# A head's q, k and guard rows together in DRAM, three V tiles moved into the score loop, the bound moved behind the last q block

## The chip, the core and the metric

The kernel runs on one core of one Trainium2 chip. The metric is the device time of one execution in microseconds (us). The engines named below are PE (TensorE), DVE (VectorE), ACT (ScalarE), POOL (GpSimd) and SP (SyncE, whose queue issues nearly all DMA transfers). The arithmetic in question is float32; matrix operands are split into a high and a low part of a shorter float type, and three products (high by high, high by low, low by high) stand in for one exact product.

## What is computed

One token block, 2048 rows of 512, goes through softmax attention with 32 heads of 16 columns, through a gated feed-forward layer of width 1792, and the two are mixed by a sigmoid gate:

```python
x = A_x                                             # 1 x 2048 x 512
g = sigmoid((x * gate_w).sum(-1, keepdims=True))
q, k, v = split(x @ wqkv)                           # 32 heads of 16
a = (softmax(q @ k.T * 16 ** -0.5) @ v) @ wo        # by head, heads side by side again
b = (silu(x @ w1) * (x @ w3)) @ w2
out = g * a + (1 - g) * b
```

## The kernel before

**First stage (lines 351 to 415).** `x` is loaded in four blocks of 512 rows, transposed on PE and split into `xH` and `xL`. For each block `project_qk` computes q and k of the first 8 heads; ACT copies the high half `hi`, DVE subtracts to get `lo`, and `store_qk` writes both to DRAM tensors of 512 rows (`QD`: qH, qL, kH, kL). `project_v` and `sums_v` compute the 16 tiles of V, twelve full-array matmuls each. `squares`, `x_squares`, `bound` and `guard_rows` work out an upper bound on the scores; two guard rows per head, written to `M_d`, become rows 48 and 49 of the q operand, so that the exponent can't overflow. If the bound is too large, a branch (`row_maxima`) computes true maxima; with these inputs it is not taken.

**The score loop (lines 849 to 880).** A string of letters fixes the order on PE. `Q` is `score`: two matmuls of 50 rows by 512 columns, one for each head of a pair, on the two halves of the array, and an exponential on ACT. `P` is `pv`: four matmuls of p with V into `acc`. `F` is `feed`: one matmul on each half of the array out of a list of other work (`blocks`: the rest of q and k, the feed-forward products, the output products). One long cycle `one` holds 8 Q, 21 F and 4 P; one short cycle `two` holds 8 Q, 15 F and 4 P. There are 90 long and 37 short cycles before the last one. A step is one pair of heads by one half of the queries, 32 Q; its operands `Qt` (q high, low, high and the guard rows: 50 rows by 1024) and `Kt` (k high, high, low: 48 rows by 2048, with rows of -1 behind them) are fetched by `load_step` one step ahead. Only the first step's operands are fetched ahead of the loop (lines 396, 401 and 409).

**The end (lines 882 to 953).** The last head pair is normalized on the spot; the last output products, eight tiles, run on PE with multiply-adds behind them and go out by DMA.

What sets the order is the program: each engine takes its instructions in the order written. On SP this holds for every DMA; each fetch or store waits there for what it needs.

Of the kernel before, what the change touches and what calls it, by code (L numbers as in the profile page):

```python
# [17 lines left out]
P = 128  # L18
# [4 lines left out]
DH = 16  # L23
NB = S // 512
# [9 lines left out]
def gated_mix_kernel(ctx: ExitStack, tc: tile.TileContext, x, wqkv, wo, w1, w3, w2, gate_w, out):  # L34
# [27 lines left out]
    qkp = ctx.enter_context(tc.tile_pool(name="qkp", bufs=1))  # L62
    fw = ctx.enter_context(tc.tile_pool(name="fw", bufs=2, side="right"))
# [3 lines left out]
    wvp = ph1.enter_context(tc.tile_pool(name="wvp", bufs=1))  # L67
# [112 lines left out]
    def x_gate(b):  # L180
        for t in range(4):
            nc.vector.scalar_tensor_tensor(slot("hx", F32), xn[b][:, t, :], 1.0, gw, op0=OP.mult, op1=OP.mult,
                                           accum_out=z[:, 4 * b + t:4 * b + t + 1])

    def store_qk(i, c, b, hi, lo):
        for t, d in zip((hi, lo), QD[i]):
            nc.sync.dma_start(d[P * c:P * c + P, 512 * b:512 * b + 512], t.bitcast(F32) if t.dtype == F32R else t)

    def project_qk(c, b, w, between=None):
        ps = psum2()  # L190
        for i in range(2):
            if i and between:
                between()
            order = [(h, xs, k) for h, xs in ((0, xH), (1, xH), (0, xL)) for k in range(ND)]
            if c == b == i == 0:
                order = [(0, xH, 0), (0, xH, 3), (0, xH, 1), (0, xH, 2), (0, xL, 0), (0, xL, 3),
                         (1, xH, 0), (1, xH, 3), (1, xH, 1), (1, xH, 2), (0, xL, 1), (0, xL, 2)]
            for n, (h, xs, k) in enumerate(order):
                nc.tensor.matmul(ps[:, i, :], w[i][h][:, k, :], xs[b][:, k, :], start=n == 0,  # L199
                                 stop=n == len(order) - 1)  # L200
        hi = p1.tile([P, 2, 512], F32R, name="hi", bufs=2)
        lo = p1.tile([P, 2, 512], F32R, name="lo", bufs=2)
        nc.scalar.activation(hi, ps, AF.Copy)
        nc.vector.tensor_sub(lo, ps, hi)
        for i in range(2):
            store_qk(i, c, b, hi[:, i, :], lo[:, i, :])
# [3 lines left out]
    def load_v():  # L210
        for k in range(ND):
            r = slot(("fh1", "fl1", "fh3", "fl3")[k], F32)
            nc.sync.dma_start(r, wqkv[P * k:P * k + P, 2 * D:3 * D])
            vh, vl = (wvp.tile([P, 512], F32R, name=f"v{n}{k}") for n in "hl")
# [37 lines left out]
    def guard_rows():  # L252
# [8 lines left out]
        for a in range(2):  # L261
            nc.sync.dma_start(M_d[:, a, :].rearrange("h (j t) -> h j t", t=512),
                              r[a][:].bitcast(F32)[:, None, :].to_broadcast([H, 4, 512]))
# [8 lines left out]
    def load_q(j, half, i):  # L272
        for h in range(2):
            r = 64 * h
            s = slice(DH * (2 * j + h), DH * (2 * j + h) + DH)
            for o, qs in enumerate((0, 1, 0)):
                nc.sync.dma_start(Qt[i][r + DH * o:r + DH * o + DH, :].bitcast(F32),
                                  QD[0][qs][s, 1024 * half:1024 * half + 1024])

    def load_guard(j, half, i):  # L280
        for h in range(2):
            nc.sync.dma_start(Qt[i][64 * h + 48:64 * h + 50, :].bitcast(F32),
                              M_d[2 * j + h, :, 1024 * half:1024 * half + 1024])

    def load_step(s):
# [3 lines left out]
        load_guard(j, half, s % 2)  # L289

    def row_maxima(small):

        with tc.If(small < 1):
# [4 lines left out]
            for j in range(NPAIR):  # L298
                load_k(j, 0)
                mx = p1.tile([P, 2, NT, 2], F32, name="mx")  # L300
                for t in range(NT):
                    if t % 8 == 0:
                        load_q(j, t // 8, 0)
# [16 lines left out]
                for h in range(2):  # L320
                    nc.sync.dma_start(M_d[2 * j + h].rearrange("a (t q) -> t a q", q=P),
# [116 lines left out]
    def qk_done(c, i, b):  # L438
        def done(ps):
# [6 lines left out]
            store_qk(i, c, b, hi, lo)  # L446
# [75 lines left out]
    def load_piece(t, q):  # L522
        if t == 1 and q < 2:
            both = wk.tile([P, 2, 512], F32R, name=f"wo{2 + q}")
# [9 lines left out]
    def load_wo(k):  # L534
        if k < 2:
            hi, lo = w2H[3][:, 2 + k, :], w2L[3][:, 2 + k, :]
        else:
            both = wk.tile([P, 2, 512], F32R, name=f"wo{k}")
# [66 lines left out]
    def divide(k, half):  # L605

        yield from reciprocals(k, half)
        for b in (2 * half, 2 * half + 1):
# [4 lines left out]
            else:  # L613
                both = wk.tile([P, 2, 512], F32, name="od")
# [12 lines left out]
    def load_bt(t):  # L627
        bt[t] = wk.tile([P, 512], F32, name=f"bt{t % 3}")
# [62 lines left out]
    def six_heads():  # L691
# [9 lines left out]
        both = wk.tile([P, 2, 512], F32, name="od")  # L701
# [13 lines left out]

    def blocks():
# [16 lines left out]
        for t in range(NT // 2, NT - 2):  # L733
            yield part_product(t, True), part_done(t), LATE
        yield part_product(NT - 2, False), (part_done(NT - 2), part_done(NT - 2)), LATE

    LATE = 3 * (ND - 1)
    NBLOCK = 8 * len(chunks) + 3 * NT + NT // 2 + NT // 2
# [4 lines left out]
    halves = [None, None]  # L743
# [7 lines left out]
    def pick(lane, rest, gap):  # L751
# [3 lines left out]
        if used < 0 or over[used] is not None and over[used] + rest <= clock:  # L755
            block, halves[lane] = halves[lane] or next(source, None), None
            if block:
                if type(block[1]) is tuple:
                    product, done, length = block
                    block, halves[1 - lane] = (product, done[0], length), (product, done[1], length)  # L760
                over.append(None)
                return dict(block=block, ps=bank(), id=len(over) - 1, n=0, turn=None, alone=halves[1 - lane] is not None or len(over) == NBLOCK)
# [78 lines left out]
    LONG, SHORT = 90, 37  # L841
# [7 lines left out]
    for i, c in enumerate(order):  # L849
        clock += 1 if c != "P" else 4  # L850
        if c == "Q":
# [14 lines left out]
            if small or later and hurry:  # L866
                for _ in range(3 if hurry else 1 + (len(small) > (6 if len(over) < 8 * len(chunks) - 16 else 0))):
                    if small or later and hurry:
                        (small or later).pop(0)()
            if loads and (hurry or issued % 2 or len(over) > 8 * len(chunks) - 12):  # L870
# [45 lines left out]
    project(last, 1, (0, 1))  # L916
# [8 lines left out]
    project(last, 1, (2,))  # L925
    project(last, 2)

    def scaled(t):
        y = wk.tile([P, 512], F32, name=f"p{free[t // 2 - 3]}")
        nc.scalar.activation(y, banks[t], AF.Copy, scale=g[:, t:t + 1])  # L930
        nc.gpsimd.tensor_add(bt[t], bt[t], y)

    def store(t):
        nc.sync.dma_start(out[P * t:P * t + P, :], bt[t])

    banks[8], banks[9] = one_[:, 1, :], two_[:, 1, :]
    banks[10], banks[11] = bank(), bank()
    for two in ((8, 9), (10, 11), (12, 13), (14,), (15,)):
        if two[0] == 12:
            banks[12], banks[13], banks[14] = psum2()[:, 0, :], psum2()[:, 0, :], acc  # L940
        for terms in ((0, 1), (2,)):
            for t in two:
                project(t, k, terms)
        for t in two:
            if t in (8, 10):
                scaled(t)
            elif t < last:
                mix(t, banks[t], nc.scalar if t % 2 == 0 else nc.sync)
                if t in (9, 11):
                    store(t - 1)  # L950
            else:
                mix(t, banks[t], nc.scalar, slice(0, D // 2))
                mix(t, banks[t], nc.sync, slice(D // 2, D))
# [27 lines left out]
```

## Time and profile before

| | |
|---|---|
| median of 3 runs | 1403.77 us (1403.39 to 1404.57) |
| profiled execution, device time | 1403.71 us |
| its span, first to last event | 1401.9 us |
| last q and k block ends, first score starts | 60.1 us, 80.97 us |
| last P group of the loop | from 1382.58 us |
| ACT, DVE, POOL busy | 1034.3, 486.9, 329.3 us |

The profiled execution's device time is 1.8 us longer than its span, and 0.06 us under the median. The times in the rows below are in us from the span's start; a row of the timeline has the start, the length, engine, line, operation, output and inputs, count, and in brackets the idle time of the engine ahead of it with what ended it.

### The profile page before, as it was taken

The page shows a single profiled execution, that of the slowest core. Times are in us where ns is not written, and L with a number is a line of the kernel's source. Part 1 is how long each engine was busy: PE and PEld are TensorE (multiplying, and loading weights), DVE is VectorE, ACT ScalarE, POOL GpSimd, SP SyncE. Part 2 cuts the span into 40 slices and gives each one's busy share as a digit, 9 for nine tenths or more (in the row PEclk, how much of TensorE's full clock was granted, in tenths as well). Part 3 has the DMA queues.
Part 4 walks back from the last instruction along what each step waited for, and adds up shares of the span by engine and source line. Part 5 has one row for each costly group of instructions (what it writes and reads, how often), then busy time and mean ns, then how long its engine had stood idle before and what let it go on. Part 6 is the DMA issues. An engine that isn't in the chain of part 4 may idle for free.

```text
span 1401.9 us, 29019 instructions
## 1 busy us (share of the span) xinstructions
PE 1393.8 (99%) x11497; PEld 826.4 (59%) x11497; DVE 486.9 (35%) x1083; ACT 1034.3 (74%) x1155; POOL 329.3 (23%) x366
## 2 busy tenths in 40 slices
PE   9999999999999999999999999999999999999998
PEld 8866566566566566566566566566555555555554
DVE  5511111564555546555454554511111101111113
ACT  4457677777777777777777777777677887888784
POOL 6123433011011101110110116432344322212312
PEclk9999999999999999999999999999999999999999
DMA  7653554343223423223333236444354453444632
GB/s 209 166 124 94 133 139 113 73 113 77 46 56 85 114 54 76 69 66 93 74 77 74 66 86 165 118 95 91 87 123 105 105 110 77 111 93 110 157 120 78
DMA packets 112479, 141.03 MB, mean 101 GB/s; under 512 B 16276, under 2 KB 70804, under 8 KB 109264
## 3 DMA queue, kind: packets, MB, share of 16 engines
q1 hardware_dynamic: 111616, 137.92, 41.4%
q8 instruction: 93, 1.52, 0.5%
q10 hardware_dynamic: 720, 1.18, 0.2%
q14 instruction: 50, 0.41, 0.1%
HBM read 90.43 MB, written 48.61 MB: 99 GB/s over the span
## 4 chain that ended last, share of the span: by engine, by line
PE 99%; DVE 0%; issue 0%; DVEq 0%
PE acc L817 33%; PE f L432 27%; PE S L829 19%; PE f L550 11%; PE f L634 2%; PE S L199 2%; PE f L641 1%; PE f L96 1%; PE f L98 1%; PE f L97 1%; PE f L165 0%; PE acc L353 0%; PE f L897 0%; PE S L165 0%; PE S L897 0%; DVE xL L646 0%
## 5 line engine op out<-in xcount | busy, mean ns | idle before, releaser
L833 ACT ACTIVATE p<-S 128x1024 f32<-128x1024 f32 x1024 | 967.9, 1026 | 314.1 <-PE S L829 305.0
L817 PE MATMUL acc<-p,V 128*17 128x512 f32 x4096 | 471.5, 594 | 0.0
L829 PE MATMUL S<-Qt,Kt 50*128 50x512 f32 x2048 | 403.7, 407 | 0.8 <-DVE V L415 0.8
L829 PEld LDWEIGHTS S<-Qt,Kt 50*128 50x128 f32 x2048 | 184.0, 184 | 173.5 <-issue 77.7
L817 PEld LDWEIGHTS acc<-p,V 128*17 128x17 f32 x4096 | 103.4, 97 | 275.2 <-issue 275.2
L463 DVE RECIPROCAL sg<-sg 128x64 f32<-128x64 f32 x448 | 209.2, 517 | 52.7 <-issue 49.1
L432 PE MATMUL f<-xH,fl 64*128 64x512 f32 x1088 | 220.6, 395 | 0.0
L432 PE MATMUL f<-xL,fh 64*128 64x512 f32 x1088 | 219.6, 393 | 0.0
L432 PE MATMUL f<-xH,fh 64*128 64x512 f32 x1088 | 218.0, 389 | 0.0
L328 POOL CAST fh<-fr 128x512 fp32r<-128x512 f32 x34 | 22.4, 658 | 428.0 <-DMA fr<-in_B_w_dram 279.6
L432 PEld LDWEIGHTS f<-xH,fh 64*128 64x128 f32 x1088 | 105.6, 184 | 25.0 <-issue 0.4
L432 PEld LDWEIGHTS f<-xL,fh 64*128 64x128 f32 x1088 | 106.4, 186 | 22.5
L432 PEld LDWEIGHTS f<-xH,fl 64*128 64x128 f32 x1088 | 106.1, 186 | 22.7
L789 DVE MEMSET tick<- 1x1 f32 x198 | 11.7, 59 | 281.2 <-PE f L550 143.0
L455 DVE COPY gs<-f 128x512 f32<-128x512 f32 x56 | 38.5, 688 | 65.5 <-PE f L432 59.3
L461 DVE TENSOR_SCALAR sg<-sg 128x512 f32<-128x512 f32 x56 | 27.3, 488 | 88.0 <-ACT sg L460 84.3
L550 PE MATMUL f<-xH,fh 64*128 64x512 f32 x208 | 57.5, 392 | 0.0
L550 PE MATMUL f<-xH,raw 64*128 64x512 f32 x192 | 57.0, 392 | 0.0
L550 PE MATMUL f<-xL,fh 64*128 64x512 f32 x208 | 56.2, 392 | 0.0
L550 PE MATMUL f<-xH,fl 64*128 64x512 f32 x208 | 55.4, 392 | 0.0
L513 POOL CAST fh<-sg 128x512 fp32r<-128x512 f32 (+1 forms) x32 | 18.0, 563 | 147.3 <-DMA sg<-h_d 91.0
L799 DVE COPY u<-acc 128x512 f32<-128x512 f32 x31 | 21.4, 692 | 86.1 <-PE acc L817 86.1
(202 smaller groups left out, 1324.6 us busy)
## 6 DMA issues: line engine op xcount, KB each, us to landing
Kt<-kH_d SPq DMA_DIRECT2D x128, 128.0 KB
h_d<-sg SPq DMA_DIRECT2D x56, 256.0 KB
sg<-h_d SPq DMA_DIRECT2D x43, 256.0 KB
fr<-in_B_w_dram SPq DMA_DIRECT2D x42, 256.0 KB
Qt<-qH_d SPq DMA_DIRECT2D x128, 64.0 KB
Kt<-kL_d SPq DMA_DIRECT2D x64, 128.0 KB
Qt<-qL_d SPq DMA_DIRECT2D x64, 64.0 KB
b_d<-y SPq DMA_DIRECT2D x16, 256.0 KB
```

What stands on the lines that cost most here:

```text
L199: nc.tensor.matmul(ps[:, i, :], w[i][h][:, k, :], xs[b][:, k, :], start=n == 0, stop=n == len(order) - 1)
L328: nc.gpsimd.tensor_copy(hi, src)
L432: return nc.tensor.matmul(ps, w[i == 1][r, k, :], (xL if i == 2 else xH)[b][r, k, :], start=n == 0 and not second, stop=n == 3 * ND - 1 an ...
L455: nc.vector.tensor_copy(gs, ps)
L461: small.append(lambda: nc.vector.tensor_scalar(sg, sg, 1.0, None, op0=OP.add))
L463: small.append(lambda q=q: nc.vector.reciprocal(sg[:, q:q + 64], sg[:, q:q + 64]))
L550: ins = nc.tensor.matmul(ps, hs[t][q][i == 1][r, P * o:P * o + P], (w2L if i == 2 else w2H)[q][r, o, :], start=n == 0 and not second, stop ...
L634: return nc.tensor.matmul(ps, ot[t][i == 1][r, P * k:P * k + P], wo_[k][i == 2][r, :], start=n == 0 and not second, stop=n == 3 * ND - 1 a ...
L799: nc.vector.tensor_copy(u, acc)
L817: nc.tensor.matmul(acc[r:r + DH + 1, :], V[:, k, 2 * j + h, :], p[:, h, :], start=k == 0, stop=k == NT - 1)
L829: nc.tensor.matmul(ps[:, h, :], Kt[i][r:r + 50, P * k:P * k + P], Qt[i][r:r + 50, t:t + 512], start=True, stop=True)
L833: nc.scalar.activation(p, ps, AF.Exp, scale=SCALE)
```

## The change

- `QD` and `M_d` go. `QX` holds for each head 50 rows of 2048: q high, q low, q high, and the two guard rows. `KX` holds 48: k high, k high, k low. `store_qk` writes the high half of q at two places, and the high half of k at two, so a block has six stores of 256 KB instead of four. Each store has the shape 8 heads by 16 rows by 512 columns; before it was 128 rows by 512.
- A step is fetched by 4 DMAs (two of 50 by 1024, two of 48 by 2048) instead of 14.
- `bound` moves ahead of V tile 9; `guard_rows` stays behind one V tile; the fetch of the first q operand moves from ahead of both to the end, since it takes the guard rows along.
- V tiles 13, 14 and 15 leave the first stage. They become the first blocks of `feed`, 24 half-array matmuls each, with a DVE copy behind each. Six short cycles become long ones (96 and 31), which gives 36 more F.
- The split weights of V stay in place for that (`wvp` is kept), and the tiles that used a later pool take their room afterwards.
- At the end, tile 13's part product is summed as two halves like tile 14's, and the last eight multiply-adds all run on DVE (before, two of them ran as an ACT scaling and a POOL add).

```diff
+EARLY = 13
-    QD = [[dram.tile([D, S], F32, name=f"{n}{p}_d") for p in "HL"] for n in "qk"]
-    M_d = dram.tile([H, 2, S], F32, name="m_d")
+    QX = dram.tile([H, 3 * DH + 2, S], F32, name="q_d")
+    KX = dram.tile([H, 3 * DH, S], F32, name="k_d")
...
-    def store_qk(i, c, b, hi, lo):
-        for t, d in zip((hi, lo), QD[i]):
-            nc.sync.dma_start(d[P * c:P * c + P, 512 * b:512 * b + 512], t.bitcast(F32) if t.dtype == F32R else t)
+    def store_qk(i, c, b, half, t):
+        for o, low in enumerate(((0, 1, 0), (0, 0, 1))[i]):
+            if low == half:
+                nc.sync.dma_start((QX, KX)[i][8 * c:8 * c + 8, DH * o:DH * o + DH, 512 * b:512 * b + 512],
+                                  t.bitcast(F32) if t.dtype == F32R else t)
...
     def load_k(j, i):
         for h in range(2):
-            r = 64 * h
-            s = slice(DH * (2 * j + h), DH * (2 * j + h) + DH)
-            for o, ks in enumerate((0, 0, 1)):
-                nc.sync.dma_start(Kt[i][r + DH * o:r + DH * o + DH, :].bitcast(F32), QD[1][ks][s, :])
+            nc.sync.dma_start(Kt[i][64 * h:64 * h + 3 * DH, :].bitcast(F32), KX[2 * j + h])
...
     project_qk(0, 3, wq)
-    load_q(0, 0, 0)
+    bound()
     project_v(9)
-    bound()
-    project_v(10)
     guard_rows()
     load_k(0, 0)
-    project_v(11)
+    load_q(0, 0, 0)
     x_gate(3)
+    project_v(10)
...
-    load_guard(0, 0, 0)
-    project_v(12)
     small = nc.values_load(flag, min_val=0, max_val=1)
-    last_v = [sums_v(t) for t in range(NT - 3, NT)]
+    last_v = [sums_v(t) for t in range(11, EARLY)]
...
+        for t in range(EARLY, NT):
+            yield v_product(t), v_done(t), 3 * ND
         for m, b in turns:
...
-    LONG, SHORT = 90, 37
+    LONG, SHORT = 96, 31
...
-    project(last, 1, (0, 1))
+    project(last, 1)
...
-    project(last, 1, (2,))
-    project(last, 2)
+    project(last, 2, (0, 1))
...
+    project(8, k, (0, 1))
+    project(last, 2, (2,))
+    project(8, k, (2,))
+    mix(8, banks[8])
```

The SP queue at the end of the first stage, before. `hi` and `lo` are the halves of q and k of the last block (the four stores of 128 rows), `sg` the guard rows, `Qt` and `Kt` the operands of the first step:

```order
L187 DMA qH_d<-hi 128x512
L187 DMA qL_d<-lo 128x512
L187 DMA kH_d<-hi 128x512
L187 DMA kL_d<-lo 128x512
L277 DMA Qt_108<-qH_d 16x1024
L277 DMA Qt_108<-qL_d 16x1024
L277 DMA Qt_108<-qH_d 16x1024 x2
L277 DMA Qt_108<-qL_d 16x1024
L277 DMA Qt_108<-qH_d 16x1024
L262 DMA m_d<-sg 32x4x512 x2
L270 DMA Kt_111<-kH_d 16x2048 x2
```

The same place now, down to the load of the flag that decides the branch:

```order
L189 DMA q_d<-hi 8x16x512 x2
L189 DMA k_d<-hi 8x16x512 x2
L189 DMA q_d<-lo 8x16x512
L189 DMA k_d<-lo 8x16x512
L267 DMA q_d<-sg 32x4x512 x2
L272 DMA Kt_108<-k_d 48x2048 x2
L276 DMA Qt_105<-q_d 50x1024 x2
L401 TENSOR_LOAD flag
```

The stores of a block are six and their leading size is 8 instead of 128, and the fetch of q, which stood ahead of the guard rows and of k, stands last.

PE behind the last q and k block, now. `S<-xL` is the end of that block, `rs` and `am` are the sums of squares that the bound is made of, `v_205` is the first of the V weights:

```order
L202 MATMUL S<-xL_586,wh 128x512 x4
L250 MATMUL f<-rs,V 1x64
L251 MATMUL f<-ident,am 1x128
L97 MATMUL f<-v_205,xH_418 128x512
L98 MATMUL f<-v_205,xH_418 128x512
```

Before, the twelve matmuls of V tile 9 stood between the block and these two (`rs` and `am` were lines 245 and 246), so the bound now asks for `am` one V tile sooner.

PE at the start of the loop, now, where the first F work is V tiles 13 and 14 instead of q and k of the next heads:

```order
L841 MATMUL S<-Qt_105,Kt_108 128x512 x4
L715 MATMUL f<-v_205,xH_585 128x512 x2
L715 MATMUL f<-v_205,xL_586 128x512 x2
L715 MATMUL f<-v_205,xH_585 128x512 x2
L715 MATMUL f<-v_210,xH_585 128x512 x2
```

The scores keep their place; the blocks that followed them move 36 F back.

More of the change, by code (lines that the diff above doesn't have):

```diff
@@ L288, in load_step @@
         load_k(j, s % 2)
-        load_guard(j, half, s % 2)
     def row_maxima(small):
@@ L714, in six_heads, with v_product, product, v_done @@
             yield
+    def v_product(t):
+        b, o = divmod(P * t, 512)
+        def product(ps, r, n, second):
+            k, i = divmod(n, 3)
+            return nc.tensor.matmul(ps, (xL if i == 1 else xH)[b][r, k, o:o + P], wv[k][i == 2][r, :],
+                                    start=n == 0 and not second, stop=n == 3 * ND - 1 and second)
+        return product
+    def v_done(t):
+        return lambda ps: nc.vector.tensor_copy(V[:, t, :, 0:DH], ps.rearrange("p (h d) -> p h d", d=DH))
     def blocks():
@@ L754, in pick @@
         used = len(over) - 3
-        if used < 0 or over[used] is not None and over[used] + rest <= clock:
-            block, halves[lane] = halves[lane] or next(source, None), None
+        if used < 0 or over[used] is not None and over[used] + (rest if len(over) < NBLOCK - 3 else 3) <= clock:
+            alone = bool(halves[lane])
+            block = halves[lane].pop(0) if alone else next(source, None)
             if block:
```

98 lines of the change are left out of this document (44 added, 54 removed).

## The prediction

> **What bounds the kernel now.** I read the page first, then PE's waits, then the chain of waits in order of time.
>
> ```profile
> PE 1393.8 (99%) x11497; PEld 826.4 (59%) x11497; DVE 486.9 (35%) x1083; ACT 1034.3 (74%) x1155; POOL 329.3 (23%) x366
> PE 99%; DVE 0%; issue 0%; DVEq 0%
> PE acc L353 <- DVE acc L349: 1.6, 1, 1.6
> PE S L829 <- DVE V L415: 0.8, 1, 0.8
> ```
>
> PE is busy 99% of the span and has two waits, 2.4 us together. So the fetches of the later steps are hidden now, and ten fewer of them per step are worth nothing by themselves. What counts is the work given to PE, and whether a new wait opens. Only the stretch ahead of the first score can open one: there the operands of the first step have no earlier step to hide behind.
>
> ```profile
> 60.11 0.39 PE L96 MATMUL f<-vh,xH 128*128 128x512 f32 x1
> 62.60 0.39 PE L98 MATMUL f<-vh,xL 128*128 128x512 f32 x1
> 80.97 0.93 PE L829 MATMUL S<-Qt,Kt 50*128 50x512 f32 x4 [0.78 <-DVE V L415]
> 813.28 3.56 PE acc L817 x32
> 1023.33 3.56 PE acc L817 x32
> 1111.96 1.84 PE acc L817 x16
> 1149.65 1.84 PE acc L817 x16
> ```
>
> The first two rows are the first and the twelfth matmul of V tile 9: 2.49 / 11 = 0.226 us each, 2.72 us a tile. The last four are P groups in the chain. Between the first pair lie 20 long cycles: 210.05 / 20 = 10.50 us. Between the second pair lie 4 short ones: 37.69 / 4 = 9.42 us.
>
> **Term 1, the loop: +6.5 us.** Six short cycles become long ones: 6 x (10.50 - 9.42) = 6.5. The 72 half-array matmuls of three V tiles fill exactly the 36 new F, so no other work gets room. ACT does not limit a long cycle: eight exponentials of 1.03 us take 8.2 of its 10.5.
>
> **Term 2, three V tiles out of the first stage: -8.2 us at most.** PE alone could start scoring at 80.97 - 3 x 2.72 = 72.8. That is worth 8.2 only if the operands have landed by then.
>
> **Term 3, when the first operands land.** First, how a store spreads over the 16 DMA engines. The trace of before has a store of the new kind: `rows` of the reciprocals goes out as 8 heads by 16 by 64 from 128 partitions. The next rows are the hardware queue's line of the DMA view, first with that store alone in the window (276 to 277.2 us), then with one old store of 128 rows (45 to 46.9 us; the row ahead of it counts its small packets).
>
> ```profile
> q1 hardware_dynamic: 136, 0.03, 12.2%
> DMA packets 145, 0.27 MB, mean 142 GB/s; under 512 B 16, under 2 KB 16, under 8 KB 144
> q1 hardware_dynamic: 144, 0.26, 35.7%
> ```
>
> Both move 128 data packets. The old store adds 16 small ones, the other only 8. I read these as one completion for each engine that takes part: 16 engines for the old stores, 8 for a store led by 8 heads. The duration of a 2 KB packet is 0.357 x 16 x 1.9 us / 128 = 85 ns, so an old store alone takes 8 x 85 ns = 0.7 us, a new one 16 x 85 ns = 1.36 us. Six of them keep eight engines for 8.2 us a block, and whatever is issued later has to pass behind them there.
>
> ```profile
> 16.81 0.33 SPq L187 DMA_DIRECT2D qH_d<-hi  x1
> 27.50 6.96 SPq L125 DMA_DIRECT2D fr<-in_A_wqkv_dram  x3
> 28.00:34.50 6.50, 6.50 (x39) 5.62 (x38) 0.31 (x1) 2.14 (x4) 6.37 (x12) 1.00 1.09 179
> 34.50:38.00 3.50, 3.50 (x17) 2.87 (x16) 2.20 (x3) 1.66 (x3) 0.52 (x1) 1.00 1.07 320
> 35.50:41.00 5.50, 5.50 (x25) 4.51 (x24) 1.91 (x2) 1.92 (x4) 0.00 (x0) 1.00 0.92 264
> 31.94 0.38 PE L165 MATMUL f<-ident,xn 128*128 128x128 f32 x2
> 41.17 0.63 ACT L238 ACTIVATE raw<-fr 128x512 f32<-128x512 f32 x1 [0.20 <-DMA fr<-in_A_wqkv_dram]
> 44.16 1.00 ACT L203 ACTIVATE hi<-S 128x1024 fp32r<-128x1024 f32 x1
> 59.45 0.17 DVE L394 TENSOR_REDUCE am<-x 128x1 f32<-128x16 f32 x1 [1.61 <-ACT sg L178]
> 60.31 1.03 ACT L203 ACTIVATE hi<-S 128x1024 fp32r<-128x1024 f32 x1 [0.89 <-PE S L199]
> ```
>
> The three window rows end with the DMA share and the rate. DMA is full from 28 us on already: the second block's stores move at 179 GB/s, the next x block at 320, the three weight pieces behind it at 264. ACT waits for the last of these pieces until 41.17. At 179 GB/s the 1.57 MB of six stores take 8.8 us, so I take 8.2 to 8.8 for a block on the eight engines. Their queue, by hand (first bytes 0.8 us behind an issue, an estimate):
>
> - block 0: from 17.6 to 25.8..26.4; x block 2 (1.05 MB at 320: 3.3) to 29.1..29.7, still ahead of its transposes at 31.94;
> - block 1's stores to 37.3..38.5; x block 3 to 40.6..41.8; three weight pieces (0.79 MB at 264: 3.0) to 43.6..44.8. Before, the last square began at 41.17, so ACT is 2.4 to 3.6 late, and `hi` of block 2 begins at 46.6..47.8 instead of 44.16;
> - block 2's stores from 1.8 behind that, 48.4..49.6, to 56.6..58.4; the next weight pieces to 59.6..61.4. From the last square to `hi` ACT needs 44.16 - 41.17 = 3.0, so `am` comes at about 62.7..64.5 instead of 59.6.
>
> The bound asks PE for `am` at 60.1: with V tile 9 no longer ahead of it, PE waits there 2.6 to 4.4 us, and the V tiles behind it wait too. Then `hi` of block 3 is 2.3 to 4.1 late, and its stores run from 64.4..66.2 to 72.6..75.0. Behind them come the guard rows, k and q.
>
> ```profile
> 67.28 0.90 SPq L262 DMA_DIRECT2D m_d<-sg  x2
> 69.00:70.00 1.00, 1.00 (x6) 0.85 (x5) 0.93 (x5) 0.60 (x1) 0.00 (x0) 1.00 1.01 207
> 71.00:76.50 5.50, 5.50 (x26) 4.57 (x25) 0.53 (x3) 0.60 (x1) 0.00 (x0) 1.00 0.88 130
> ```
>
> The guard rows (0.52 MB at 207 GB/s) take 2.5 us; the part that lies on the other eight engines is hidden, so 2. The fetch of k took 6.0 us at 130 GB/s in pieces of 16 rows. Pieces of 48 rows do not occur before; their bounds are 2.5 (the 320 of the x block) and 6.0, and I take 3.5, since the x block's 128 rows are the nearest wide transfer. The q fetch, 0.41 MB, must wait for the guard rows in DRAM, which the old one did not; its bounds are 1.3 (at 320) and 3.2 (at 130), I take 2. With 0.5 for two landings the first score starts at 80.6..83.0, **82 taken**, and with both ends of the unknown fetches and of a block's stores it is 78..87. Against 80.97 that is +1.0 (-3 to +6). So term 2 is lost whole: PE is through with its four V tiles at 62.7..64.5 + 4 x 2.72 + 0.7 = 74.3..76.1 and then idles about 6 us.
>
> The Trainium skill, "DMA: Bandwidth & Descriptors", section "Why a DMA increments its semaphore by 16 and not by 1", has a transfer run on the largest number up to 16 that divides both leading sizes. For 8 heads by 128 rows that is 8, as the small packets say; for the 50-row fetch of q, which no row here shows, it would be 10, and the sum would be about 1 us higher, an estimate.
>
> **Term 4, the clock: +2.2 us.** A wait of this length is new to PE, and the trace shows what follows one.
>
> ```profile
> 1.55 3.01 PE L353 MATMUL acc<-ident 128*128 128x128 f32 x13 [1.55 <-DVE acc L349]
> 7.19 1.26 PE L353 MATMUL acc<-ident 128*128 128x128 f32 x10
> 1396.00:1398.00 2.00, 0.12 (x1) 0.00 (x0) 1.43 (x3) 0.00 (x0) 0.00 (x0) 1.00 1.01 377
> 1398.00:1399.00 1.00, 0.00 (x0) 0.00 (x0) 0.00 (x0) 0.00 (x0) 0.00 (x0) 0.81 1.01 377
> 1399.00:1400.00 1.00, 0.00 (x0) 0.00 (x0) 0.00 (x0) 0.00 (x0) 0.00 (x0) 0.50 0.73 260
> ```
>
> PE ends at 1396.12; the granted clock is 1.00 up to 1398, 0.81 on average in the next us, and 0.50 after that, so it falls to half at about 1398.6, 2.5 us after the last matmul. At the start the same transposes take 0.23 us each, by 7.19 they take 0.13: about 4.5 us at half speed. If PE idles 6 us ahead of the first score, the loop begins so, and 4.5 us at half speed cost 2.2. The bounds are 0 (data by 2.5 us after the V tiles) and 4.5 (the same at the bound, if that is not hidden behind the data).
>
> The Trainium skill, "TensorE: Matmul & The Clock Gate", section "Part 1: The HAM clock gate", gives about 3.4 us both for idling and for warming up; by it this term would be 1.7 instead of 2.2. The trace's 2.5 and 4.5 decide here.
>
> **Term 5, the end: +0.3 us.**
>
> ```profile
> 1386.07 0.50 PE L641 MATMUL f<-wo,xL 64*128 64x512 f32 x1
> 1386.40 0.39 PE L641 MATMUL f<-wo,xH 64*128 64x512 f32 x1
> 1390.61 0.69 DVE L924 TENSOR_TENSOR xL<-acc,xH 32x512 fp32r<-32x512 f32 x1
> 1394.58 1.41 DVE L646 SCALAR_TENSOR_TENSOR xL<-S,g,xL 128x512 f32<-128x512 f32 x2 [0.38 <-PE S L897]
> 1396.56 0.87 DVE L646 SCALAR_TENSOR_TENSOR xL<-f,g,xL 128x256 f32<-128x256 f32 x2
> ```
>
> One more half-array matmul is left over behind the loop, 0.33. All eight tiles now end in a DVE add: from 1391.30, 7 x 0.75 + 0.9 gives 1397.45, as before (1396.56 + 0.87 = 1397.43). So only the delay counts. The stores leave one by one as before.
>
> **Sum:** +1.0 + 6.5 + 2.2 + 0.3 = +10.0 us on the profiled execution's 1403.71, which is 0.06 under the median of the runs: **1413.7 us**, 0.7% slower. With the ends of its terms this case reaches from 1406.5 (first score at 78, no clock loss) to 1419. The edits to pools, names and the order of the next blocks I cost at nothing: the first chunk's weights and the q and k stores of the next heads have a whole step of 32 Q, some 42 us, ahead of them.
>
> **The rivals.**
>
> - **The new stores cost nothing extra per byte** (they spread over 16 engines after all). Then the first stage keeps its pace, `hi` of block 3 is ready at 61.3, its stores end about 66.2, guard rows 68.8, k 72.3, q 74.3, and the first score starts at about 74.7: -6.3 + 6.5 + 0.3 = +0.5, 1404.2. For it speaks that both kinds move the same 2 KB packets; against it the 8 small packets. Chance 0.14.
> - **Not slower: the first operands beat PE.** The wider fetch of k and the shorter SP queue bring everything by 72.8. Then -8.2 + 6.5 + 0.3 = -1.4, 1402.3. It decides at a first score before 74.4, where -6.6 pays for the loop and the end. For it speaks that 48 rows are fetched at once; against it that 1.57 MB of stores, 0.52 of guard rows and 1.19 of fetches follow each other through DRAM from 62 us on, 3.3 MB that even at 320 GB/s last until 72.3, with two landings to be waited for in between. Chance 0.06.
> - **The delays pile up.** If ACT is late enough with `hi` of block 2, V tiles 5 and 6 are copied late and PE stalls at the transposes of block 3 (50.11 us) as well; the first score comes at 86 or later, with clock losses in two places: +5.5 + 6.5 + 4.5 + 0.3 = +16.8, 1420.5. Slack for it is about 1 us by the rows above. Chance 0.10.
> - The main case has 0.70.
>
> **Chances and range.** A measurement can tell about 0.2%, 2.8 us, from no change. Slower by more than that: the main case, the pile-up, and a little of the first rival, 0.82. Within: 0.13. Faster: even the second rival gives only -1.4, so 0.05. The range runs from the first rival to the top of the main case, 1404 to 1419.
>
> **What would show it.** Right: a PE wait for `am` of some us at the bound, a wait of the first score for the q fetch, a granted clock of 0.5 there, new stores with 8 small packets, 96 long cycles of 10.50 us, no wait for a fetch later in the loop. Wrong: first scores before 78 us, no wait at the bound, or cycles of another length; a gain in the loop itself would mean that the fetches were not hidden.

## The result, and the profile after

The changed kernel takes 1451.54 us (median of 6 runs, 1447.45 to 1452.2) against 1403.81 us (6 runs, 1403.11 to 1404.7): a ratio of 1.0335, 95% interval 1.0322 to 1.0348. The direction was forecast, the size was not: 47.7 us instead of 10, far above the range.

From the page of the changed kernel, the span, the busy time of each engine and the shares of the chain that ended last:

```profile
span 1448.8 us, 28719 instructions
PE 1407.5 (97%) x11533; PEld 835.1 (58%) x11533; DVE 489.4 (34%) x1090; ACT 1032.5 (71%) x1151; POOL 325.3 (22%) x364
PE 85%; DMA 5%; issue 1%; POOL 1%; SPq 1%; DVE 0%; DVEq 0%; POOLq 0%
```

Before, the chain was 99% PE. Now 5% of it is DMA: at several places PE ran out of work and a transfer was what came last. PE's longest waits in the changed kernel (us in total, times, longest):

```profile
PE f L422 <- DVE tick L801: 13.8, 4, 4.9
PE S L841 <- SPq L286: 10.0, 1, 10.0
PE f L250 <- DVE rs L244: 5.7, 1, 5.7
PE f L541 <- POOL fr L504: 3.1, 1, 3.1
...
PE f L251 <- DVE am L387: 1.5, 1, 1.5
```

Two of them lie in the first stage at the bound (L250, L251), one ahead of the first score (L841), four in the loop's q and k blocks (L422), one at the switch to the h products (L541). The groups of P matmuls in the chain say whether the cycles themselves are as forecast (start, length, what):

```profile
342.45 3.56 PE acc L829 x32
352.95 3.56 PE acc L829 x32
...
1148.09 1.84 PE acc L829 x16
1150.60 1.84 PE acc L829 x16
1157.52 1.84 PE acc L829 x16
```

A long cycle is still 10.5 us, a short one 9.43 (1157.52 - 1148.09). So the loop at rest is unchanged, and the time went into a few places. To place it, each cycle is counted from one eighth exponential of a score (the ACT row that writes p) to the next. The profiled execution of every run below is cut at the same points and compared with before: the start of the first exponential (81.8 us before), the first 40 cycles (which hold the q and k blocks), cycles 41 to 88 (which hold the switch to the h products), and the rest (six more long cycles, and the end).

| run | span, us | first exponential | cycles 1 to 40 | cycles 41 to 88 | rest | sum |
|---|---|---|---|---|---|---|
| the change | 1448.8 | +11.0 | +22.9 | +7.6 | +5.4 | +46.9 |
| layout_only | 1432.3 | +12.4 | +19.1 | 0.0 | -1.2 | +30.4 |
| vmove_only | 1418.9 | -1.1 | +2.0 | +9.8 | +6.3 | +17.0 |
| four_stores_8 | 1405.0 | +1.2 | +2.0 | 0.0 | -0.1 | +3.1 |
| six_stores_128 | 1414.2 | +6.9 | +5.4 | +0.1 | -0.1 | +12.3 |
| six_stores_8 | 1435.3 | +11.0 | +22.4 | +0.1 | 0.0 | +33.4 |
| six_stores_pitch | 1402.3 | +0.2 | +0.4 | 0.0 | -0.1 | +0.4 |
| six_stores_pad | 1402.3 | 0.0 | +0.4 | 0.0 | -0.1 | +0.3 |
| six_stores_8_pitch | 1432.2 | +11.1 | +19.3 | 0.0 | -0.1 | +30.3 |
| change_pitch | 1448.0 | +9.0 | +23.8 | +7.9 | +5.4 | +46.1 |
| third_buffer | 1414.2 | +11.7 | +1.5 | +0.6 | -1.5 | +12.3 |
| column_layout_only | 1404.3 | +2.2 | +1.5 | +0.1 | -1.4 | +2.4 |
| rows_by_column | 1417.0 | -1.4 | +1.1 | +8.7 | +6.6 | +15.1 |
| vmove_shift | 1410.4 | -1.3 | +1.8 | +1.4 | +6.6 | +8.5 |
| vmove_bound_shift | 1410.3 | -1.8 | +2.6 | +1.4 | +6.1 | +8.4 |
| column_shift | 1410.0 | -2.1 | +2.0 | +1.1 | +7.0 | +8.0 |

In the change nearly all of the 22.9 us of the first 40 cycles is three cycles of 17.5 us (they begin at 146, 206 and 256 us) where 10.5 is normal. The chain in order of time shows what stands at the first of them (start, length, what):

```profile
147.34 7.45 DMA k_d<-gs
...
154.82 0.05 DVEq L433
...
154.91 0.06 DVE gs L433
```

PE's timeline has the matmul that waited, with its idle time in brackets:

```profile
155.75 0.79 PE L422 MATMUL f<-xH,fl 64*128 64x512 f32 x2 [4.70 <-DVE tick L801]
```

DVE's timeline has what PE waited for:

```profile
140.88 0.69 DVE L433 COPY gs<-f 128x512 f32<-128x512 f32 x1 [1.38 <-PE f L422]
...
154.91 0.69 DVE L433 COPY gs<-f 128x512 f32<-128x512 f32 x1 [6.80 <-DMA k_d<-gs]
155.54 0.06 DVE L801 MEMSET tick<- 1x1 f32 x1
```

and the windows view has the stretch around the end of that wait (window, PE, PEld, DVE, ACT and POOL busy, granted clock, DMA share, GB/s; the granted clock is the share of full speed at which the matmuls run):

```profile
153.50:160.30 6.80, 4.55 (x22) 2.85 (x26) 0.75 (x3) 1.70 (x2) 1.89 (x2) 0.50 0.72 173
```

It reads backwards. PE waits for `tick`, a memset of 0.06 us that the kernel sets between the two halves of a block, since both halves of the array write the same bank of results in turn. The `tick` stands on DVE behind the copy of a finished block (L433), which moves the block out of its bank. The copy waits for one of the two `gs` buffers, from which POOL makes the two halves and SP stores them. That buffer is held by a store to `k_d`, issued at 147.34, which takes 7.45 us to land. The buffer was filled from 140.88 on, so it was held for 13.9 us: 6.5 until its last store was issued, 7.45 until that had landed. PE stands still for 4.70 us, from 151.05 to 155.75, and the granted clock is 0.50 from 153.5 to 160.3: 4.55 us of matmuls at half speed lose another 2.3. Together that is the 7.0 us.

DVE's waits between 85 and 300 us, of the change and then of before, tell the same in sum:

```profile
DVE gs L433 <- DMA q_d<-gs: 29.6, 4, 10.8
DVE gs L433 <- DMA k_d<-gs: 23.7, 5, 6.8
```

```profile
DVE gs L443 <- DMA kL_d<-gs: 11.0, 3, 5.4
DVE gs L443 <- DMA qL_d<-gs: 4.8, 2, 3.0
```

The wait for the buffer was there before, 15.8 us of it, and reached PE nowhere; now it is 53.3 and does.

### The profile page after: what moved, and what is told of

Read it like the earlier page. It is cut to its first block, busy times and chain, and to the rows that moved or that the text cites. A ratio compares the mean times of both kernels' runs of the same rounds, so it can differ in the third digit from the quotient of the medians.

```text
span 1448.8 us, 28719 instructions
## 1 busy us (share of the span) xinstructions
PE 1407.5 (97%) x11533; PEld 835.1 (58%) x11533; DVE 489.4 (34%) x1090; ACT 1032.5 (71%) x1151; POOL 325.3 (22%) x364
## 4 chain that ended last, share of the span: by engine, by line
PE 85%; DMA 5%; issue 1%; POOL 1%; SPq 1%; DVE 0%; DVEq 0%; POOLq 0%
PE acc L829 30%; PE f L422 24%; PE S L841 17%; PE f L541 10%; PE f L629 2%; DMA q_d<-sg 1%; DMA q_d<-gs 1%; PE f L636 1%; DMA k_d<-gs 1%; DMA fr<-in_B_w_dram 1%; PE f L715 1%; DMA sg<-h_d 0%; SPq L189 0%; PE f L909 0%; POOL gs L435 0%
## 5 line engine op out<-in xcount | busy, mean ns | idle before, releaser
L841 PE MATMUL S<-Qt,Kt 50*128 50x512 f32 x2048 | 407.4, 409 | 10.0 <-SPq L286 10.0
L841 PEld LDWEIGHTS S<-Qt,Kt 50*128 50x128 f32 x2048 | 186.7, 186 | 179.3 <-issue 92.0
L422 PE MATMUL f<-xH,fl 64*128 64x512 f32 x1088 | 220.8, 398 | 13.8 <-DVE tick L801 13.8
L422 PE MATMUL f<-xL,fh 64*128 64x512 f32 x1088 | 219.0, 395 | 0.0
L422 PE MATMUL f<-xH,fh 64*128 64x512 f32 x1088 | 217.1, 391 | 0.0
L422 PEld LDWEIGHTS f<-xH,fl 64*128 64x128 f32 x1088 | 105.1, 187 | 38.4 <-DVE tick L801 10.4
L422 PEld LDWEIGHTS f<-xH,fh 64*128 64x128 f32 x1088 | 104.7, 186 | 25.0
L422 PEld LDWEIGHTS f<-xL,fh 64*128 64x128 f32 x1088 | 105.7, 188 | 22.6
L541 PE MATMUL f<-xH,fh 64*128 64x512 f32 x208 | 58.1, 393 | 0.0
L541 PE MATMUL f<-xH,raw 64*128 64x512 f32 x192 | 56.4, 392 | 0.0
L541 PE MATMUL f<-xL,fh 64*128 64x512 f32 x208 | 56.1, 392 | 0.0
L541 PE MATMUL f<-xH,fr 64*128 64x512 f32 x160 | 51.8, 395 | 3.9 <-POOL fr L504 3.1
L541 PE MATMUL f<-xH,fl 64*128 64x512 f32 x208 | 55.3, 394 | 0.0
```

The costliest lines, as they stand in the source:

```text
L422: return nc.tensor.matmul(ps, w[i == 1][r, k, :], (xL if i == 2 else xH)[b][r, k, :], start=n == 0 and not second, stop=n == 3 * ND - 1 an ...
L541: ins = nc.tensor.matmul(ps, hs[t][q][i == 1][r, P * o:P * o + P], (w2L if i == 2 else w2H)[q][r, o, :], start=n == 0 and not second, stop ...
L841: nc.tensor.matmul(ps[:, h, :], Kt[i][r:r + 50, P * k:P * k + P], Qt[i][r:r + 50, t:t + 512], start=True, stop=True)
```

## The experiments

Theory A, formed on this: a store led by 8 heads runs on half of the DMA engines, and six of them a block hold the buffers too long. Its rivals: the 50% more bytes alone, the shape of the new fetches, and the V tiles with another alignment of work.

### Layout and V tiles apart

The layout alone: the change with these lines back as before, and the bound and the V tiles of the first stage back in their old order. The new end stays, in this run as in the next.

```diff
-EARLY = 13
+EARLY = 16
...
-    LONG, SHORT = 96, 31
+    LONG, SHORT = 90, 37
```

> The changed kernel with V tiles 13 to 15 back in the first stage, the bound in its old place and the old end (90 and 37 long and short cycles): the new rows in DRAM, the six stores a block led by 8 heads and the four fetches a step are left as the change has them. Theory A (each store led by 8 heads runs on half of the DMA engines, and six of them a block hold the two-deep store buffers gs and sg so long that DVE's next copy, the PSUM bank and then PE wait): the loop's stalls of the q and k blocks stay, about 20 us over 14 cycles, and the first score is late by some 5 to 10 us for the late stores, with nothing given back but the three V tiles: 1425 to 1445. Theory B (the V tiles and the place of the bound cause it, by another alignment of blocks and loads): 1402 to 1408. The stall of 7.5 us at the switch to the h products (between 940 and 990 us) stays by A's buffers if it is the layout's, and goes if it is an alignment that the three V blocks shift.

Measured: 1431.16 us, ratio 1.0194 (1.0177 to 1.0211). And the V tiles alone, the change with

```diff
-    QX = dram.tile([H, 3 * DH + 2, S], F32, name="q_d")
-    KX = dram.tile([H, 3 * DH, S], F32, name="k_d")
+    QD = [[dram.tile([D, S], F32, name=f"{n}{p}_d") for p in "HL"] for n in "qk"]
+    M_d = dram.tile([H, 2, S], F32, name="m_d")
```

and the stores, fetches and the bound's place of before:

> The kernel before with its rows in DRAM, four stores of 128 rows a block and 14 fetches a step, and with the bound in its old place, but with V tiles 13 to 15 as blocks between scores, 96 and 31 cycles and the new end. Theory A: the first stage gets shorter by up to 8.2 us for the three tiles (less where the operands of the first score are then late), the loop longer by 6.5, and nothing else: 1400 to 1406. Theory B: most of the 47 us, 1435 to 1452. If the stall of 7.5 us at the switch to the h products is an alignment of blocks and loads, it shows here too, and the time is 1407 to 1414.

Measured: 1420.87 us, 1.0130 (1.0113 to 1.0147), above theory A's range and the one for an alignment at the switch, and far below theory B's. By the table the two halves are nearly additive (30.4 + 17.0 = 47.4), and each has its own places: the late start and the stalls of the q and k blocks are the layout's, the stall behind 930 us and the longer cycles are the V move's. The V move also shows that three tiles fewer ahead of the loop bring almost nothing (the first score in its timeline):

```profile
79.58 1.42 PE L850 MATMUL S<-Qt,Kt 50*128 50x512 f32 x4 [7.48 <-SPq L295]
```

PE is through with its V tiles some 8 us earlier, at about 72.1, and then waits 7.48 us.

### Number of stores and their lead

In the kernel before, with its 14 fetches and V tiles: two more stores a block (`XD` is written and read by nobody), or the lead of 8 heads, or both. With the lead of 8 each head has a 17th row that is not used, so that the rows of two heads do not lie next to each other and merge into one run of 128.

```diff
-        for t, d in zip((hi, lo), QD[i]):
+        for t, d in zip((hi, hi, lo), (QD[i][0], XD[i], QD[i][1])):
```

```diff
-    QD = [[dram.tile([D, S], F32, name=f"{n}{p}_d") for p in "HL"] for n in "qk"]
+    QD = [[dram.tile([H, DH + 1, S], F32, name=f"{n}{p}_d") for p in "HL"] for n in "qk"]
...
-            nc.sync.dma_start(d[P * c:P * c + P, 512 * b:512 * b + 512], ...)
+            nc.sync.dma_start(d[8 * c:8 * c + 8, 0:DH, 512 * b:512 * b + 512], ...)
```

> The kernel before with two more stores a block, the high halves of q and k once more into rows that nobody reads: six stores of 128 rows each in place of four, so the bytes of the change with the packets of before. Theory A: the two stores cost SP some 0.8 us of issue a block and little else; first score 0 to 4 us later, loop stalls below 5 us: 1404 to 1412. Volume theory (50% more bytes and issues are what holds the buffers, however they are spread): the loop's stall of some 20 us and the first score 5 to 10 us late, 1425 to 1445.

> The kernel before with its four stores a block led by 8 heads (a head's 16 rows lie 17 rows apart from the next head's, so that the rows of two heads don't merge), the same bytes and the same fetches. Theory A (the spread over half of the engines counts): the stores take about twice as long to land, first score 2 to 5 us late, loop stalls of the q and k blocks 4 to 15 us: 1410 to 1425. Volume theory: within 2 us of before, 1402 to 1406.

> The kernel before with its 14 fetches a step, and six stores a block (the high halves of q and k once more into rows that nobody reads), all led by 8 heads. Alone, two more stores cost 12.3 us and the lead of 8 heads 3.2. Theory A2 (both together pass what the eight engines can take, and a queue builds up): as the layout alone, 1425 to 1436, with stalls near 146, 206 and 256 us. Theory B2 (what the layout costs beyond that comes from its four large fetches, whose 48 and 50 rows queue with the stores): the two prices add up, 1417 to 1422, and the loop's stalls stay below 9 us.

Measured: six_stores_128 1415.48 us, 1.0082 (1.0065 to 1.0099); four_stores_8 1407.90, 1.0030 (1.0018 to 1.0041); six_stores_8 1435.88, 1.0222 (1.0205 to 1.0239). The first two fell between the ranges of both theories, so A was restated as A2 ahead of the third run, and that came out as A2 had it: alone they cost 12.3 and 3.1 us, both together 33.4 us, with cycles of 16.7 to 17.9 us that begin at 146, 206 and 255 us, just as in the change. The fetches are still 14 there, so the stalls do not need the shape of the new fetches.

### Rows by column

The three rows of a head's column lie side by side, so that a store of 8 heads by 16 columns becomes one of 128 rows; once in the change, once in the layout alone (6 fetches a step, guard rows apart).

```diff
-    KX = dram.tile([H, 3 * DH, S], F32, name="k_d")
+    KX = dram.tile([H, DH, 3, S], F32, name="k_d")
...
-                nc.sync.dma_start((QX, KX)[i][8 * c:8 * c + 8, DH * o:DH * o + DH, 512 * b:512 * b + 512],
+                nc.sync.dma_start((QX, KX)[i][8 * c:8 * c + 8, :, o, 512 * b:512 * b + 512].rearrange("h d t -> (h d) t"),
```

> The changed kernel with the three rows of each of a head's 16 columns side by side in DRAM (row 3 x column + part), so that each of the six stores is led by 128 rows again; q and k are fetched as 48 rows, and the guard rows lie apart, 6 fetches a step. V tiles, bound and cycles as in the change. Theory A2: the loop's stalls of the q and k blocks fall from 22.8 us to the 5 of six stores on all engines, and the first exponential comes at 80 to 90 us in place of 92.8; the stall at the switch to the h products (7 to 9 us) and the 6.5 us of short cycles stay: 1415 to 1428. Theory B2 (the large fetches): 1435 to 1450.

> The layout alone (V tiles, bound and end as before the change), with the three rows of a head's column side by side, so that the six stores a block are led by 128 rows; 6 fetches a step. Theory A2: what the layout cost (27.5 us) goes but for a remainder: first exponential 82 to 86 us, loop stalls 0 to 3 us, 1403 to 1410. If two more stores a block cost what they cost beside 14 fetches (12.3 us): 1413 to 1418.

Measured: rows_by_column 1418.17 us, 1.0102 (1.0085 to 1.0118); column_layout_only 1407.25, 1.0024 (1.0014 to 1.0034). Same bytes, same number of stores: the layout's 27.5 us shrink to 3.3. The DMA view shows why, as busy tenths of the 16 engines in 40 slices of a window of 35 us with q and k blocks; first the change (130 to 165 us), then column_layout_only (120 to 155 us):

```profile
DMA  5564555889555557431244566699793544555555
GB/s 194 171 173 126 185 204 201 280 222 273 148 178 180 162 183 215 155 84 26 49 37 169 185 225 87 194 293 215 164 178 56 220 180 183 204 204 199 201 204 197
```

```profile
DMA  9998019920211100899999998899999960000079
GB/s 375 365 379 330 0 47 379 377 96 7 56 40 38 47 0 0 311 377 304 281 229 192 197 215 133 211 370 403 396 337 258 258 204 6 0 0 0 0 264 382
```

By column the stores come as short peaks at about 370 GB/s with all engines busy, and gaps between them. In the change there is a plateau at 5, half of the engines, near 190 GB/s, that leaves no gap: one block's stores run into the next one's. Counted from the packets of 2 KB between 90 and 300 us: of the time in which any was under way, exactly 8 were at once in 67.9 of 129.1 us in the change; by column 16 were the commonest number, 26.8 of 81.1 us.

### Distance of the rows, and what the lead costs without it

By column the rows also lie 24 KB apart in place of 8 KB, so two things had changed. In six_stores_128 alone, without any change of lead:

```diff
-    QD = [[dram.tile([D, S], F32, name=f"{n}{p}_d") for p in "HL"] for n in "qk"]
+    QD = [[dram.tile([D, 3, S], F32, name=f"{n}{p}_d") for p in "HL"] for n in "qk"]
```

(only part 0 is used; six_stores_pad has `[D, S + 512]` instead), and the same third dimension under the lead of 8 heads, in six_stores_8 and in both tensors of the change:

```diff
-    KX = dram.tile([H, 3 * DH, S], F32, name="k_d")
+    KX = dram.tile([H, 3 * DH, 3, S], F32, name="k_d")[:, :, 0, :]
```

> The kernel before with six stores of 128 rows a block and 14 fetches a step, as the run that cost 12.3 us, but the rows of every q and k tensor lie 24 KB apart in place of 8 KB, as they do by column. Six stores by column cost 3.4 us only, and a 2 KB packet took 91 ns there against 139 ns here. If it is the distance of the rows: packets of 85 to 105 ns, and 1404 to 1409. If it is the 14 fetches a step, with their issue on SP: packets of 125 to 145 ns, and 1412 to 1418.

> Six stores of 128 rows a block and 14 fetches, with rows 10 KB apart (512 columns of padding). If any distance other than 8 KB will do: packets of 85 to 105 ns and 1403 to 1408, as with 24 KB. If it takes more than that: 1408 to 1418.

> Six stores a block led by 8 heads and 14 fetches a step (1435.9 us with rows 8 KB apart), with the rows of every q and k tensor 24 KB apart. If the distance of the rows makes the price: no stall in the loop, first exponential at 82 to 86 us, 1403 to 1410. If the lead of 8 heads does: packets stay near 100 ns, 8 at a time, stalls of 15 us or more, 1425 to 1436. If both have a part (eight engines at full rate carry six stores just so): 1410 to 1425.

> The changed kernel with nothing else than rows 24 KB apart in both tensors. If the distance makes the price: first exponential at 80 to 85 us, no stalls of q and k blocks, and the stall at the switch (8 us), the short cycles (6.5) and the cold first cycle stay: 1414 to 1422, as by column. If the lead does: 1440 to 1452.

Measured: six_stores_pitch 1404.08 us, 1.0003 (0.9993 to 1.0012); six_stores_pad 1404.01, 1.0002 (0.9993 to 1.0012); six_stores_8_pitch 1433.39, 1.0201 (1.0184 to 1.0218); change_pitch 1451.15, 1.0345 (1.0327 to 1.0362). Under a lead of 128 rows the distance is everything: two more stores cost 12 us at 8 KB and nothing that can be measured at 10 or 24 KB. Under a lead of 8 heads it hardly counts: the changed kernel stays at 1451. So the layout's price in the change is that of the lead with six stores a block. PE's waits of six_stores_8_pitch are those of the change again:

```profile
PE f L433 <- DVE tick L790: 11.5, 4, 4.6
PE S L830 <- SPq L294: 4.8, 1, 4.8
PE f L246 <- DVE rs L240: 3.0, 1, 3.0
PE f L247 <- DVE am L395: 1.6, 1, 1.6
```

### A third buffer

In layout_only, with nothing changed about the stores:

```diff
-            lo = slot("gs", F32)
-            hi = slot("sg")
+            lo = slot(("gs", "gs", "hx")[qk_left % 3], F32)
+            hi = slot(("sg", "sg", "gw")[qk_left % 3])
```

> The layout alone as the change has it (stores led by 8 heads), with a third buffer for the low and for the high half of q and k blocks, in tiles that are idle at that time; the stores and their bytes stay. If the two-deep buffers turn a burst of slow stores into a wait of PE: the loop's 19.1 us of stalls fall by a third or more, to 4 to 13 us, and the time to 1416 to 1425; the late first exponential stays at 94. If the eight engines are simply short of rate over the whole stretch of q and k blocks, a third buffer only puts the wait off: 17 to 20 us of stalls, 1428 to 1433.

Measured: 1416.78 us, 1.0096 (1.0080 to 1.0111). PE's waits of this run:

```profile
PE S L843 <- SPq L286: 5.2, 1, 5.2
PE f L250 <- DVE rs L244: 3.0, 1, 3.0
PE acc L346 <- DVE acc L342: 1.6, 1, 1.6
PE f L251 <- DVE am L387: 1.5, 1, 1.5
```

The wait of the q and k blocks (`f` at the place of L422) is gone, 19.1 us of the loop became 1.5, more than was expected; the late start stays at 93.5 us. The eight engines carry the stores on the average, then; it is the bursts that two buffers do not cover.

### The stall at the switch to the h products

In the V move alone, and then with the bound moved too, and in the change with rows by column, one step's fetches are put off:

```diff
-            if issued % 32 == 6 and step < 2 * NPAIR:
+            if issued % 32 == (18 if step == 21 else 6) and step < 2 * NPAIR:
```

> The V tiles moved alone, with one difference: the 14 fetches of step 21 are issued 12 scores later (about 15 us), so that they no longer stand on the SP queue ahead of the fetches of h at the switch to the h products. If the stall of 9.5 us in the cycle at 934 us is this alignment: 1410 to 1413. If it is the place of the blocks themselves (POOL's splits, the buffers of h): as before the shift, 1419 to 1422.

The second also has the bound ahead of V tile 9:

```diff
-    project_v(9)
     bound()
-    project_v(10)
+    project_v(9)
     guard_rows()
     load_k(0, 0)
     x_gate(3)
+    project_v(10)
```

> The same, with the bound ahead of V tile 9 as in the change (old rows in DRAM). The first score waits 7.5 us in the V move alone, for SP, behind the guard rows' way through DRAM, which starts one V tile earlier now: the first exponential comes 2 to 4 us earlier, 1406 to 1411 if the shift works, 1415 to 1420 if it does not. If the wait is for the stores and fetches of q and k rather than for the guard rows, nothing is gained by the bound: 1410 to 1413.

> The changed kernel with rows by column (1418.2 us) and with step 21's fetches 12 scores later. The stall of 8.4 us in the cycle at 933 us goes, as it went in the V move alone (8.3 us): 1408 to 1411. What is left over before would then be the 6.5 us of six longer cycles and the slower first cycle.

Measured: vmove_shift 1412.55 us, 1.0066 (1.0049 to 1.0082); vmove_bound_shift 1411.45, 1.0057 (1.0040 to 1.0073); column_shift 1411.95, 1.0055 (1.0041 to 1.0069). The cycle at 934 us goes from 19.99 to 11.02 us in the V move, and from 18.89 to 11.35 by column. The timeline of SP and PE in vmove_only shows the order that does it; the second fence is SP in vmove_shift:

```profile
932.04 0.37 SPq L512 DMA_DIRECT2D sg<-h_d  x1
932.51 0.45 SPq L279 DMA_DIRECT2D Qt<-qH_d  x1
...
938.40 0.57 SPq L284 DMA_DIRECT2D Qt<-m_d  x2
939.07 9.67 SPq L512 DMA_DIRECT2D sg<-h_d  x4
...
945.91 0.79 PE L550 MATMUL f<-xH,fr 64*128 64x512 f32 x1 [6.07 <-POOL fr L513]
```

```profile
931.49 8.74 SPq L512 DMA_DIRECT2D sg<-h_d  x4
940.33 0.75 SPq L279 DMA_DIRECT2D Qt<-qH_d  x1
```

The three V blocks move everything behind them later by 36 F, and so the first pieces of h fall just behind a step's 14 fetches on SP's queue: 939.07 instead of 931.49. POOL splits them late, and PE waits 6.07 us for the split. In the change the new rows make it 4 fetches, and it stalls all the same, in the same cycle (the shift was tried by column, with 6 fetches, and not in the change itself):

```profile
965.07 0.78 SPq L276 DMA_DIRECT2D Qt<-q_d  x2
965.91 1.24 SPq L272 DMA_DIRECT2D Kt<-k_d  x2
968.38 10.19 SPq L503 DMA_DIRECT2D sg<-h_d  x4
```

The bound ahead of V tile 9 brings the first exponential only 0.6 us earlier (80.6 to 80.0), below the 2 to 4 that were expected, and the time lies in the range that was given for a wait on the stores and fetches of q and k. The last run, 1411.95, lies just above its 1408 to 1411. No version of the layout or of the V move came out ahead of the kernel before: what is left in column_shift, +8.0 us, is the rest of the loop and the end (+7.0, with the longer cycles), a slower beginning of the loop (+2.1) and 1.1 in the middle, against 2.1 won at the start.

## Why the prediction was wrong

- **The step that failed** is the last sentence of the sum: the q and k stores of the loop were costed at nothing, since "a whole step of 32 Q, some 42 us" lies ahead of their use. That looked at who reads the rows. It did not ask who waits for the store itself: the store holds `gs` and `sg`, two deep, and the copy of a later block stands behind them, on DVE the `tick` behind that copy, and PE behind the `tick`. The copies of these blocks in the kernel before (count, shortest, median and longest in ns, first and last start):

```profile
L443 DVE COPY gs<-f x24: 691/692/694, 93.8 to 226.4; 128x512 f32<-128x512 f32 x24
```

  One comes every 5.8 us (132.6 / 23), so two buffers cover 11.5 us less the work between, not 42. In the change this cost about 21 us, three cycles of 17.5 instead of 10.5, and six stores a block led by 8 heads bring the same stalls into the kernel before (six_stores_8); a third buffer takes the loop's loss from 19.1 to 1.5 us. "No wait for a fetch later in the loop" held for the fetches only. Of the 37.7 us between forecast and result these 21 are the largest part; term 3 has some 10 and the switch to the h products 7.6. Whether PE would have been spared with the `tick` on another engine was not tried.
- **The spread over 8 engines** (term 3's base) was right, and is shown by the runs: under the lead of 8 a distance of 24 KB leaves 30.3 of 33.4 us (six_stores_8_pitch), and the lead of 128 mends it. The Trainium skill, "DMA: Bandwidth & Descriptors", section "Why a DMA increments its semaphore by 16 and not by 1", says it so (the largest number up to 16 that divides both leading sizes); the 8 packets at once agree. The rival that denied it is refuted.
- **Term 3 was mis-sized**: +1.0 us forecast (at most +6), +10.7 measured for the first score (91.68 against 80.97). The chain of causes was right, each link longer. Third square of the first weights at 45.70 instead of 41.17 (4.5 late; 2.4 to 3.6 forecast), `am` at 68.53 instead of 59.45 (9.1 late; 3.3 to 5.1 forecast), PE's wait at the bound 5.70 + 1.47 = 7.2 us (2.6 to 4.4 forecast):

```profile
45.70 0.63 ACT L243 ACTIVATE raw<-fr 128x512 f32<-128x512 f32 x1 [0.18 <-DMA fr<-in_A_wqkv_dram]
63.74 0.63 ACT L243 ACTIVATE raw<-fr 128x512 f32<-128x512 f32 x1 [7.39 <-DMA fr<-in_A_wqkv_dram]
68.53 0.17 DVE L387 TENSOR_REDUCE am<-x 128x1 f32<-128x16 f32 x1 [1.76 <-ACT sg L179]
91.68 1.42 PE L841 MATMUL S<-Qt,Kt 50*128 50x512 f32 x4 [10.00 <-SPq L286]
```

- **Term 2** (-8.2 at most) was indeed lost whole, but not for the stores' sake alone. With all engines on the stores the first score still comes at 79.33 us (rows_by_column), 9.2 us after the last of its fetches was issued:

```profile
70.16 0.54 SPq L282 DMA_DIRECT2D Qt<-m_d  x2
79.33 1.42 PE L849 MATMUL S<-Qt,Kt 50*128 50x512 f32 x4 [6.43 <-DVE V L413]
```

  The rival with 16 engines had 74.7 there, and its 1404.2 would have been wrong as well: the way of the last block through DRAM or the branch behind the bound limits the start even with the lead of 128. Which of the two takes how much was not tried.
- **Term 1** was right: 96 long cycles of 10.50 us, short ones of 9.43, +6.5. What it left out is that 36 more F also shift the switch to the h products: +7.6, the V move's second price, and removed by shifting one step's fetches.
- **Term 4** was right in kind and a little large: the loop begins at a clock of 0.50 and the first cycle is 11.64 us against 10.34, +1.3 instead of +2.2. It falls to 0.50 at the bound too (from 64.7 to 71.6 us), where PE then waits 10.0 us for the first score all the same; whether it delayed the guard rows, which need a matmul behind V tile 9, was not tried. The clock falls again behind each stall of the loop (2.3 us at the one shown above), which no term had. **Term 5** had the wrong sign: in all runs with the new end the span ends 14.3 to 14.6 us after the last P matmul, in those with the old end 15.6 to 15.8. So the end gained about 1.2 us where +0.3 was forecast.
- **The rival in which delays pile up** had the late first score (86 or later), but by a stall at the transposes of block 3 that is not among PE's waits, and its 1420.5 is far off as well.
- **Slips in the sums**, none of which made the miss: by its own terms the low end of the main case is 1407.5 (-3 + 6.5 + 0.3), and its bounds for the fetches give a first score from 78.9, not 78; the upper end takes 2.2 for the clock, whose own bound was 4.5; the loop and the end need 6.8 us to be paid for, a first score before 74.2, not 74.4.

## What to carry to other kernels

When a store gets slower, ask first what its source buffer is for and how soon that is wanted again, and only then when the data is read back; the cover is the depth of the buffer times the time between blocks. When a layout changes, look at the leading dimension that the DMA sees on both sides: 128 rows as 8 x 16 are the same bytes at half the engines, and a dimension order that merges them again gave 24 us back. A wait on one engine also holds what stands behind it there, however short that is. Blocks put into a fixed order shift all that follows, so look for the next place where queues meet (here 36 F later at the h products), and try moving the neighbour's fetches before giving up the move.

## What was not expected of the hardware

Stores of 128 rows by 2 KB into rows 8 KB apart in DRAM ran slower than into rows 10 or 24 KB apart. A 2 KB packet (loads of 2 KB rows included) took 139 ns on the average between 90 and 300 us in six_stores_128, 92 in six_stores_pad and 91 in six_stores_pitch, which differ in that distance alone; it is worth 12 us of the kernel's time. The Trainium skill, "DMA: Bandwidth & Descriptors", section "Latency and other measured facts", lists such a loss for copies within DRAM at distances of 512 KiB and more, and a padding of 4 KiB as its cure there; here 2 KB of padding at 8 KB was enough. Why it is so was not tried. In the kernel before, with four stores 8 KB apart, the packets took 106 ns, and its time is the same as that of six stores with padding, so there the slower packets cost nothing.
